# Gated rows transposed on VectorE in 32x32 squares with transfers inside SBUF, and the output's products moved behind the sixth product

## The chip, the cores and the metric

The kernel runs on one core of one Trainium2 chip. The metric is the device time of one execution in microseconds (us), the median of the runs. For a single execution the hardware profiler gives a trace, from which all the rows below come.

## The reference

One block of a network on 2048 rows of 512 columns, in f32: an attention part, then a gated part, each with a normalisation ahead and an addition to its input behind.

```python
h = x + _A_ref(_layernorm(x, axis=-1), A_wqkv, A_wo)
h2 = h + _B_ref(_layernorm(h, axis=-1), B_w_in, B_w_sp, B_b_sp, B_w_out)

def _B_ref(x, w_in, w_sp, b_sp, w_out):
    z = _gelu(jnp.einsum("bsd,df->bsf", x, w_in))
    z1 = z[..., :Fh]                                  # Fh = 688
    z2 = _layernorm(z[..., Fh:], axis=-1)
    g = jnp.einsum("ts,bsf->btf", w_sp, z2) + b_sp[None, :, None]
    return jnp.einsum("bsf,fd->bsd", z1 * g, w_out)
```

The change is in the last two lines: the product of w_sp (2048x2048) with z2 (2048x688), the gate z1 * g, and the product of the gated rows with w_out (688x512).

## The kernel before

All large products are made from fp16 halves: an f32 operand is split into a part rounded to fp16 (`hi`) and the rest (`lo`), and hi x hi, hi x lo and lo x hi are summed in PSUM (`mm3`, lines 106 to 109; their matmuls carry lines 107, 108 and 109 everywhere).

The last stage (lines 1413 to 1512) runs over eight pairs of row blocks, `p` = 0 to 7; a pair is the blocks p and p + 8 of 128 rows each (`w` = 0 and 1, "top" and "bottom"). In each pair:

- Seven products of one 1024-deep sum and 344 columns give g for both blocks (a Strassen-like scheme). They run in the order b11, t1, t2, b22, t3, b21, n4, each of 24 matmuls (`product`, which also asks for a left operand `op` eight products ahead, by SyncE). They accumulate in PSUM tiles A, C and B.
- VectorE and ScalarE combine the sums, GpSimd multiplies with z1. This makes the gated rows `pr`, two blocks of 688 columns in f32: right of top behind b22, right of bottom (`br`) behind t3, left of top behind b21, left of bottom (`bl`) behind n4.
- The columns are handled in two halves: half 0 is the columns 0 to 383, half 1 the rest. `level` finds each row's largest magnitude in a half (VectorE), `raise_` scales the half by a power of two (ScalarE, in place), `lower` makes the factors that undo it.
- The output's product needs the gated rows with columns along the partitions. `turn` transposes three 128x128 tiles on TensorE into PSUM, `split` reads them there into fp16 `pT` hi (ScalarE) and lo (VectorE), `multiply` makes one 128x512 output product from three tiles (9 matmuls for half 0, 8 for half 1) in a PSUM tile `acc`, `gather` scales it and adds it to the rows of h (VectorE), `store` writes them out.

The tiles `acc` come from a pool of two (`ps_o`, `bufs=2`). The order of instructions on each engine is the order of the code (a manual schedule), each engine takes its queue strictly in order, and semaphores connect the engines. In the code before, half 1 of a pair is turned behind its product n4, its output products (`multiply(1, w)`) stand behind the next pair's b11, followed there by the turn of half 0, whose output products stand behind the next pair's t1. The last pair has its own tail at lines 1497 to 1512, and it turns half 1 ahead of n4.

Of the kernel before, what the change touches and what calls it, by code (L numbers as in the profile page):

```python
# [8 lines left out]
F32 = mybir.dt.float32  # L9
F32R = mybir.dt.float32r  # L10
BF = mybir.dt.bfloat16
F16 = mybir.dt.float16
I32 = mybir.dt.int32
AF = mybir.ActivationFunctionType
# [5 lines left out]
P = 128  # L20
# [4 lines left out]
FH = 688  # L25
# [15 lines left out]
HF = 3 * P  # L41
# [18 lines left out]
def block_kernel(ctx: ExitStack, tc: tile.TileContext, x, wqkv, wo, w_in, w_sp4, b_sp, w_out, out):  # L60
# [7 lines left out]
    nc = tc.nc  # L68
# [26 lines left out]
    def split(hi, lo, src, eh=None, el=None):  # L95

        if eh == "act":
            nc.scalar.activation(hi, src, AF.Copy)  # L98
        elif eh == "pool":
            nc.gpsimd.tensor_copy(hi, src)  # L100
        else:
            nc.vector.tensor_copy(hi, src)
        back = hi if hi.dtype == F16 else hi.bitcast(F32)
        (nc.gpsimd if el == "pool" else nc.vector).tensor_sub(lo, src, back)  # L104
# [164 lines left out]
    with ExitStack() as pre:  # L269
# [244 lines left out]
        kf, accs, rest, measures = {}, [0], [], []  # L514
# [96 lines left out]
        for g in range(3):  # L611
            a, b = 4 * g, 4 * g + 4
# [54 lines left out]
        for j in range(24):  # L667
            b, n, i = 1 + j // 8, j // 2 % 4, 1 - j % 2
# [117 lines left out]
    with ExitStack() as at:  # L786
# [13 lines left out]
        def product(s, hg, qb, kb, p, t):  # L800

            r = slice(RG * t, RG * t + KM)
            nc.tensor.matmul(s, kst[hg % 2][r, p, kb * P:(kb + 1) * P],  # L803
                             qst[hg * NQ + qb][r, p, :], start=True, stop=True)
# [122 lines left out]
        def send():  # L927
            for i, key in enumerate(measured):
                nc.sync.dma_start(top_scr.rearrange("o (p i) -> (o p) i", i=4)[:, i:i + 1],
                                  sizes_of[key][:, :1])  # L930
# [112 lines left out]
        for n in range(0, len(units), 2):  # L1043
# [53 lines left out]
            for tok in PAIR if len(later) < 2 else ():  # L1097
                i = int(tok[-1]) if tok[-1].isdigit() else 0
# [16 lines left out]
                elif tok == "H":  # L1115
                    a = 0 if first else 256
# [47 lines left out]
    with ExitStack() as mid:  # L1164
# [5 lines left out]
        def turn(sb):  # L1170

            hn = hns.pop(sb)
            tp = pt.tile([P, DB, P], F32, name="tp")
            for d in range(DB):
                nc.tensor.transpose(tp[:, d, :], hn[:, d * P:(d + 1) * P], ident)
            hTs[sb] = [m2.tile([P, DB, P], F16, name=f"hT{i}") for i in range(2)]
            split(hTs[sb][0], hTs[sb][1], tp, "act")
# [107 lines left out]
    with ExitStack() as fin:  # L1285
# [3 lines left out]
        f2 = fin.enter_context(tc.tile_pool(name="fin_2", bufs=2))  # L1289
# [5 lines left out]
        def next_g():  # L1295
            banks[0] += 1
            return ps_g[(banks[0] - 1) // 2 % 2].tile([P, 512], F32, name="g")[:, :FC]

        TW = P // 2
# [38 lines left out]
        class Rows:  # L1338
# [26 lines left out]
            def lower(self, half, *which):  # L1365

                for w in which:
                    d = self.downs[half, w]
                    nc.vector.tensor_scalar(d, d, 2.0 ** -14, w_down, op0=ALU.mult, op1=ALU.mult)

            def turn(self, half, w):

                if half:
                    nc.gpsimd.tensor_copy(self.pr[:, w, FH:], self.pr[:, w, FH - TW:FH])
                tp = self.turned[half, w] = ps_t.tile([P, 512], F32, name="tp").rearrange(
                    "p (i t) -> p i t", t=P)
                for i in range(3):
                    c = min(HALVES[half].start + i * P, FH - TW)
                    nc.tensor.transpose(tp[:, i, :], self.pr[:, w, c:c + P], ident)

            def split(self, half, w):

                tp, n = self.turned.pop((half, w)), 3 - half
                if half not in self.pT:
                    self.pT[half] = [f2.tile([P, 2, 3, P], F16, name=f"pT{half}{i}") for i in range(2)]
                hi, lo = self.pT[half]
                nc.scalar.activation(hi[:, w], tp[:, :3], AF.Copy)
                nc.vector.tensor_sub(lo[:, w, :n], tp[:, :n], hi[:, w, :n])
                if half:
                    t = hi[TW:, w, n]  # L1390
                    nc.vector.tensor_sub(t, tp[TW:, n], t)
# [33 lines left out]
        with tc.manual_schedule(engines={E.PE, E.Activation, E.DVE, E.Pool, E.SP}):  # L1425
            wu = [f1.tile([P, 2 * 3, D], F16, name=f"wu{i}") for i in range(2)]
            raw_w = f1.tile([P, 2 * 3, D], F32, name="raw_w")
            w_top, w_low, w_up, w_down = [f1.tile([P, n], F32, name=f"w_{i}") for i, n in enumerate((6, 1, 1, 1))]
            nc.gpsimd.memset(raw_w[:, 2 * 3 - 1, :], 0.0)
            nc.sync.dma_start(raw_w[:, :5, :], w_out[:5 * P, :].rearrange("(i p) c -> p i c", p=P))  # L1430
            for r0 in (TW - fn, P - fn):
                nc.sync.dma_start(raw_w[r0:r0 + fn, 5, :], w_out[5 * P:, :])
            nxt = fetch(0)
            now = None
            for p in range(HB):
                (z1t, z1b, ht, hb), last = nxt, p + 1 == HB
                nxt = None if last else fetch(p + 1)
                before, now = now, Rows(p, (ht, hb))
                bt, bb = bias_up[:, p:p + 1], bias_up[:, p + HB:p + HB + 1]
                A, C, B = [next_g() for _ in range(3)]  # L1440
                p1, v, q5 = [f0.tile([P, FC], F32, name=n) for n in ("p1", "v", "q5")]
                left, right = now.pr[:, 0, :FC], now.pr[:, 0, FC:FH]
                bl, br = now.pr[:, 1, :FC], now.pr[:, 1, FC:FH]

                product(A, "b11")
                nc.scalar.activation(p1, A, AF.Identity, bias=bt)
                if p:
                    accs = [before.multiply(1, w) for w in range(2)]
                    for w in range(2):
                        before.turn(0, w)  # L1450
                        before.gather(1, w, accs[w])
                        before.split(0, w)
                    before.lower(0, 0, 1)
                product(C, "t1")
                nc.scalar.activation(q5, C, AF.Identity, bias=bb)
                if p:
                    accs = [before.multiply(0, w) for w in range(2)]
                    for w in range(2):
                        before.gather(0, w, accs[w])
                        before.store(w)  # L1460
                else:
                    weigh_w()
                product(A, "t2", False)
                nc.scalar.activation(v, A, AF.Identity, bias=bt)
                product(C, "b22", False)
                nc.vector.tensor_add(right, C, v)  # L1466
                nc.gpsimd.tensor_mul(right, right, z1t[:, FC:])  # L1467
                if not p:
                    measure_w()
                product(A, "t3", False)  # L1470
                nc.vector.tensor_add(br, A, q5)
                (nc.vector if last else nc.gpsimd).tensor_mul(br, br, z1b[:, FC:])
                now.level(1, 0, 1)
                now.raise_(1, 0, 1)
                product(B, "b21")
                nc.vector.tensor_add(left, B, p1)
                (nc.vector if last else nc.gpsimd).tensor_mul(left, left, z1t[:, :FC])
                if last:
                    now.level(0, 0)
                    for w in range(2):  # L1480
                        now.turn(1, w)
                        now.split(1, w)
                    now.lower(1, 0, 1)
                    now.raise_(0, 0)
                product(A, "n4", False)
                nc.vector.scalar_tensor_tensor(bl, A, bb, z1b[:, :FC], op0=ALU.add, op1=ALU.mult)
                if last:
                    now.level(0, 1)
                    now.raise_(0, 1)
                else:  # L1490
                    now.level(0, 0, 1)
                    for w in range(2):
                        now.turn(1, w)
                        now.split(1, w)
                    now.lower(1, 0, 1)
                    now.raise_(0, 0, 1)
            accs = [now.multiply(1, 0)]
            now.turn(0, 0)
            now.split(0, 0)
            accs.append(now.multiply(1, 1))  # L1500
            now.turn(0, 1)
            now.gather(1, 0, accs[0])
            now.split(0, 1)
            now.gather(1, 1, accs[1])
            now.lower(0, 0, 1)
            acc = now.multiply(0, 0)
            now.gather(0, 0, acc)
            now.store(0)
            acc = now.multiply(0, 1)
            for c in (slice(0, D // 2), slice(D // 2, D)):  # L1510
                now.gather(0, 1, acc, c)
                now.store(1, c)
# [29 lines left out]
```

## Time and profile before

| what | us |
|---|---|
| median of 3 runs (1726.46 to 1728.48) | 1726.86 |
| the profiled execution's own time | 1726.86 |
| its span, first to last instruction | 1725.10 |
| TensorE busy | 1708.8 (99%) |
| VectorE busy | 1438.4 (83%) |
| ScalarE busy | 1318.7 (76%) |
| GpSimd busy | 815.5 (47%) |

In the rows, PE is TensorE, DVE VectorE, ACT ScalarE, POOL GpSimd and SPq the queue of SyncE, which issues the transfers. A timeline row has the start, the duration, the engine, the line of the kernel, the instruction, the tile written and the tiles read, the shapes, and in brackets how long the engine had been idle and who ended that. A row by line has the count, the busy time and the mean of one in ns, then the idle time ahead. A row of a stretch has for each engine the busy time and the number of instructions in it, then the granted TensorE clock, the share of the DMA engines and GB/s. Matmul rows overlap, so TensorE's own pace is read from start to start. The last stage lies between 1455 and 1725 us.

### The profile page before, as it was taken

What the parts mean: (1) busy time and instruction counts of PE and PEld (TensorE: products, weight loads), DVE (VectorE), ACT (ScalarE), POOL (GpSimd) and SP (SyncE); (2) the same over time, 40 slices, a digit from 0 to 9 for tenths busy, and PEclk for the clock granted to TensorE, in tenths of its full rate; (3) what the DMA queues carried; (4) which work ended last, traced back from release to release, by engine and by line L of the source; (5) the groups of instructions that cost most, each with busy time, mean ns of one, the idle gap of its engine ahead of it and who ended that gap; (6) DMA issues with size and microseconds to landing.
All of it is one profiled execution on the core that took longest, in us unless ns stands there. A gap on an engine that the chain in (4) does not pass through costs nothing.

```text
span 1725.1 us, 36747 instructions
## 1 busy us (share of the span) xinstructions
PE 1708.8 (99%) x13583; PEld 653.4 (38%) x13583; DVE 1438.4 (83%) x3030; ACT 1318.7 (76%) x2598; POOL 815.5 (47%) x1076
## 2 busy tenths in 40 slices
PE   9999999999999999999999999999999999999999
PEld 4433222222222222222222222222216566666665
DVE  7688999999999999999999999999927886433234
ACT  4334999999999999999999999999994554221111
POOL 1231867776672267687677866400013766110010
PEclk9999999999999999999999999999999999999999
DMA  5534332342231234344345343300124464654540
GB/s 183 162 97 144 101 88 69 100 98 81 75 71 27 60 105 117 113 149 135 103 121 146 115 147 103 80 20 12 45 51 135 136 184 159 228 179 145 170 139 25
DMA packets 183932, 190.51 MB, mean 110 GB/s; under 512 B 65704, under 2 KB 134632, under 8 KB 183752
## 3 DMA queue, kind: packets, MB, share of 16 engines
q1 hardware_dynamic: 181448, 182.53, 36.2%
q10 hardware_dynamic: 2304, 5.64, 0.8%
q8 instruction: 106, 1.74, 0.4%
q14 instruction: 74, 0.61, 0.1%
HBM read 122.10 MB, written 65.93 MB: 109 GB/s over the span
## 4 chain that ended last, share of the span: by engine, by line
PE 76%; DVE 15%; DMA 3%; ACT 2%; issue 2%; POOL 2%; SPq 1%; DVEq 0%; ACTq 0%; POOLq 0%
PE pv L828 26%; PE s L803 17%; PE m L223 9%; DVE mx L228 7%; PE acc L107 4%; PE g L109 4%; PE g L108 4%; PE g L107 4%; PE acc L109 3%; PE acc L108 3%; DVE ab L237 1%; DMA rc<-r_scr 1%; DVE og L838 1%; DVE rs_t L124 1%; DVE rs_u L126 1%
## 5 line engine op out<-in xcount | busy, mean ns | idle before, releaser
L812 ACT ACTIVATE pt<-s 128x512 f32<-128x512 f32 x1968 | 1006.3, 637 | 5.1 <-PE m L223 4.0
L228 DVE TENSOR_REDUCE mx<-m 128x1 f32<-128x512 f32 x1510 | 947.5, 682 | 12.6 <-PE m L223 3.9
L803 PE MATMUL s<-qst,kst 50*128 50x512 f16 x2048 | 604.3, 379 | 0.2
L828 PE MATMUL pv<-pt,vst 128*32 128x256 f32 (+1 forms) x6056 | 598.1, 466 | 4.1 <-DVE og L838 1.3
L223 PE MATMUL m<-kst,qst 48*128 48x512 f16 x1510 | 452.4, 381 | 0.0
L803 PEld LDWEIGHTS <-kst 50*128 50x128 f16 x2048 | 131.9, 94 | 352.1 <-issue 323.7
L828 PEld LDWEIGHTS pv<-pt,vst 128*32 128x32 f32 x6056 | 119.5, 108 | 290.3 <-issue 276.9
L223 PEld LDWEIGHTS <-qst 48*128 48x128 f16 x2048 | 159.2, 93 | 173.7 <-issue 124.3
L223 PE MATMUL m<-uvs,qst 48*128 48x512 f16 x504 | 190.5, 380 | 0.3 <-DVE mx L228 0.3
L245 POOL TENSOR_SCALAR nm<-nm 128x16 f32<-128x16 f32 x32 | 6.6, 206 | 359.7 <-DVE nm L242 359.7
L237 DVE CUSTOM_DVE_ANT_0 ab<-m,ab 128x512 f32<-128x512 f32 x252 | 170.5, 677 | 2.7 <-ACT ab L233 2.7
L233 ACT ACTIVATE ab<-m 128x512 f32<-128x512 f32 x252 | 157.3, 624 | 16.5 <-PE m L223 15.8
L989 POOL TENSOR_TENSOR op<-raw,op 128x512 f16<-128x512 f32 x80 | 92.9, 1161 | 6.0
L1467 POOL TENSOR_TENSOR pr<-pr,z 128x344 f32<-128x344 f32 x8 | 7.3, 912 | 176.9 <-DVE pr L1466 173.0
L912 POOL TENSOR_TENSOR raw<-raw 128x512 f32<-128x512 f32 (+1 forms) x84 | 83.3, 991 | 6.7
L917 POOL TENSOR_TENSOR acc_sp<-acc_sp,raw 128x512 f32<-128x512 f32 x63 | 80.5, 1277 | 4.5
L107 PE MATMUL acc<-wi,hT 128*128 128x344 f16 x256 | 79.1, 309 | 1.4 <-ACT hT L98 1.4
L1362 ACT ACTIVATE pr<-pr,up 128x304 f32<-128x304 f32 (+1 forms) x32 | 17.0, 574 | 81.9 <-DVE up L1316 81.9
L109 PE MATMUL acc<-wi,hT 128*128 128x344 f16 x256 | 79.1, 309 | 0.3 <-DVE hT L104 0.3
L108 PE MATMUL acc<-wi,hT 128*128 128x344 f16 x256 | 79.1, 309 | 0.0
L1408 DVE SCALAR_TENSOR_TENSOR h<-acc,low,h 128x512 f32<-128x512 f32 (+1 forms) x33 | 24.1, 732 | 45.8 <-PE acc L109 32.5
L909 POOL TENSOR_SCALAR raw<-raw 128x512 f32<-128x512 f32 (+1 forms) x88 | 52.3, 594 | 19.5 <-DMA raw<-in_wqkv 12.2
(240 smaller groups left out, 2280.1 us busy)
## 6 DMA issues: line engine op xcount, KB each, us to landing
raw<-in_w_sp SPq DMA_DIRECT2D x128, 256.0 KB
s_scr<-op SPq DMA_DIRECT2D x64, 256.0 KB
op<-s_scr SPq DMA_DIRECT2D x32, 512.0 KB
a_scr<-op SPq DMA_DIRECT2D x48, 256.0 KB
op<-a_scr SPq DMA_DIRECT2D x24, 512.0 KB
o_scr<-og SPq DMA_DIRECT2D x64, 128.0 KB
qst<-q_scr SPq DMA_DIRECT2D x192, 32.0 KB
kst<-k_scr SPq DMA_DIRECT2D x48, 128.0 KB
```

The source lines that it names most:

```text
L107: nc.tensor.matmul(ps, lh, rh, start=first, stop=False, **kw)
L108: nc.tensor.matmul(ps, lh, rl, start=False, stop=False, **kw)
L109: nc.tensor.matmul(ps, ll, rh, start=False, stop=last, **kw)
L223: nc.tensor.matmul(acc, q[r, p, c], keys[r, p], start=True, stop=True)
L228: nc.vector.reduce_max(at(t, e if t else e - 1), acc, axis=AX.X)
L233: nc.scalar.activation(ab[0], acc, AF.Abs)
L237: nc.vector.tensor_tensor_reduce(ab[0], acc, ab[0], 0.5, LOW, ALU.add, ALU.max, at(0, 0))
L803: nc.tensor.matmul(s, kst[hg % 2][r, p, kb * P:(kb + 1) * P], qst[hg * NQ + qb][r, p, :], start=True, stop=True)
L812: nc.scalar.activation(pts[p, kb][:, t, :], s, AF.Exp, scale=scales_[hg // 2])
L828: nc.tensor.matmul(pv[0][32 * j:32 * j + 32, a:b], vst[hg % 2][:, c:c + 32], pts[j % 2, kb][:, j // 2, a:b], start=kb == 0, stop=kb == NB - 1,
L912: pool.tensor_mul(got[0] if n else acc, got[0], got[0])
L989: chores.append((lambda: pool.tensor_sub(t[0][:, 1], of(), t[0][:, 0]), TT))
```

## The change

For all pairs but the last, the transposition leaves TensorE and PSUM:

- `squares(half)` transposes the scaled rows on VectorE in squares of 32x32, from `pr` into an SBUF tile `squares`. In half 1 these are four instructions (two of 256 columns, two of 2x64), issued behind the scaling that follows t3; in half 0 one instruction of 768 columns, behind the scaling that follows n4.
- `send` puts the squares in their places with 16 transfers from SBUF to SBUF, each of 32 partitions with 384 elements, issued by SyncE into a tile `whole`.
- `hi` and `lo` split `whole` into the fp16 tiles: ScalarE copies 768 columns for each half (behind b22 of the next pair), VectorE subtracts with four instructions (behind t3 of the next pair, ahead of `level`).
- All four output products stand behind b21 of the next pair and ahead of n4, half 1 first; `store` stands behind n4.
- The last pair is turned by TensorE as before. Its `turn` of half 1 now stands between the two halves of pair 6's output products.

```diff
+            def squares(self, half):
+                if half:
+                    self.sq = f2.tile([P, 4, 2, 2, 3, 32], F32, name="squares", bufs=1)
+                t = self.sq[:, :, half]
+                if half:
+                    for w in range(2):
+                        nc.vector.transpose(t[:, :, w, :2].rearrange("p q i a -> p i q a"),
+                                            self.pr[:, w, HF:HF + 2 * P])
+                    for q in (0, 2):
+                        nc.vector.transpose(t[:, q:q + 2, :, 2].rearrange("p q w a -> p w q a"),
+                                            self.pr[:, :, FH - TW:FH])
+                else:
+                    nc.vector.transpose(t.rearrange("p q w i a -> p (w i) q a"), self.pr[:, :, :HF])
+            def send(self):
+                self.whole = f2.tile([P, 4, 2, 2, 3, 32], F32, name="whole", bufs=1)
+                for j in range(4):
+                    for q in range(4):
+                        nc.sync.dma_start(self.whole[32 * q:32 * q + 32, j], self.sq[32 * j:32 * j + 32, q])
+            def hi(self, half):
+                src = self.whole[:, :, half].rearrange("p j w i a -> p (w i) j a")
+                self.pT[half] = [f2.tile([P, 2, 3, P], F16, name=f"pT{half}{i}", bufs=1) for i in range(2)]
+                nc.scalar.activation(self.pT[half][0].rearrange("p w i (j a) -> p (w i) j a", a=32), src, AF.Copy)
...
                 product(A, "b11")
                 nc.scalar.activation(p1, A, AF.Identity, bias=bt)
-                if p:
-                    accs = [before.multiply(1, w) for w in range(2)]
-                    for w in range(2):
-                        before.turn(0, w)
-                        before.gather(1, w, accs[w])
-                        before.split(0, w)
-                    before.lower(0, 0, 1)
                 product(C, "t1")
...
                 (nc.vector if last else nc.gpsimd).tensor_mul(br, br, z1b[:, FC:])
+                if p:
+                    before.lo(1)
+                    before.lo(0)
                 now.level(1, 0, 1)
                 now.raise_(1, 0, 1)
+                if not last:
+                    now.squares(1)
                 product(B, "b21")
                 nc.vector.tensor_add(left, B, p1)
                 (nc.vector if last else nc.gpsimd).tensor_mul(left, left, z1t[:, :FC])
+                if p:
+                    accs = [before.multiply(1, w) for w in range(2)]
+                    for w in range(2):
+                        before.gather(1, w, accs[w])
...
+                if p:
+                    accs = [before.multiply(0, w) for w in range(2)]
+                    for w in range(2):
+                        before.gather(0, w, accs[w])
                 product(A, "n4", False)
...
                     now.level(0, 0, 1)
-                    for w in range(2):
-                        now.turn(1, w)
-                        now.split(1, w)
-                    now.lower(1, 0, 1)
                     now.raise_(0, 0, 1)
+                    now.squares(0)
+                    now.send()
```

On VectorE, in a middle pair, this is the queue from the addition behind t3 to the one behind n4 as it was (`pr<-g,q` is the addition behind t3, `pr<-g,p` the one behind b21):

```order
L1471 TENSOR_TENSOR pr<-g,q_23975 128x344
L1351 TENSOR_REDUCE low_24173<-pr 128x2
L1313 TENSOR_SCALAR low_24173<-low_24173 128x2
L1314 TENSOR_SCALAR low_24173<-low_24173 128x2
L1316 TENSOR_SCALAR up_24174<-low_24173 128x2
L1476 TENSOR_TENSOR pr<-g,p_23973 128x344
L1486 SCALAR_TENSOR_TENSOR pr<-g,fig_1843,z_23660 128x344
```

And this is the queue from the addition behind t3 to the first gather of an output product (`h<-acc`) in the changed kernel:

```order
L1508 TENSOR_TENSOR pr<-g,q_24284 128x344
L1410 TENSOR_TENSOR pT_24399<-whole,pT_24398 128x256 x2
L1412 TENSOR_TENSOR pT_24398<-whole,pT_24398 64x2x128
L1406 TENSOR_TENSOR pT_24402<-whole,pT_24401 128x768
L1351 TENSOR_REDUCE low_24436<-pr 128x2
L1313 TENSOR_SCALAR low_24436<-low_24436 128x2
L1314 TENSOR_SCALAR low_24436<-low_24436 128x2
L1316 TENSOR_SCALAR up_24437<-low_24436 128x2
L1378 STREAM_TRANSPOSE squares<-pr 128x2x4x32 x2
L1381 STREAM_TRANSPOSE squares<-pr 128x2x2x32 x2
L1518 TENSOR_TENSOR pr<-g,p_24282 128x344
L1451 SCALAR_TENSOR_TENSOR h_23666<-acc,low_24132,h_23666 128x512
```

Four subtractions stand ahead of the maximum, four transpositions ahead of the addition behind b21, and the gathers follow that addition.

On TensorE, before, at the border of two pairs the six transposes stand between n4 and b11:

```order
L108 MATMUL g<-n_1_20677,op 128x344
L109 LDWEIGHTS op
L109 MATMUL g<-n_0_20676,op 128x344
L1379 MATMUL tp<-ident,pr 128x128 x6
L107 LDWEIGHTS op
L107 MATMUL g<-b_0_20664,op 128x344
```

In the changed kernel they are gone there. This is the place behind b21 where the second output product ends and the third begins (pT_23790 is half 1, pT_23793 half 0):

```order
L1446 LDWEIGHTS pT_23790
L1446 MATMUL acc<-wu_23068,pT_23790 128x512
L107 LDWEIGHTS pT_23793
L107 MATMUL acc<-wu_23067,pT_23793 128x512
L108 LDWEIGHTS pT_23793
L108 MATMUL acc<-wu_23068,pT_23793 128x512
```

The output products of the two halves, which had the six transposes and t1 between them, now follow each other directly.

On SyncE, the 16 transfers stand behind the stores of the pair before and ahead of the loads for the next pair but one, in the changed kernel:

```order
L1161 DMA op<-a_4_scr 128x2048
L1454 DMA out_y<-h_23090 128x512
L1454 DMA out_y<-h_23092 128x512
L1391 DMA whole<-squares 32x384 x16
L1464 DMA z_23966<-z_scr 128x688
L1464 DMA z_23968<-z_scr 128x688
L1464 DMA h_23970<-h_scr 128x512
L1464 DMA h_23972<-h_scr 128x512
L1161 DMA op<-s_4_scr 128x2048 x4
```

The loads of z and h, which stood at the start of the pair behind the seventh `op`, now wait in the queue behind the squares.

More of the change, by code (lines that the diff above doesn't have):

```diff
@@ L1369, in lower, with lo @@
                     nc.vector.tensor_scalar(d, d, 2.0 ** -14, w_down, op0=ALU.mult, op1=ALU.mult)
+            def squares(self, half):
[20 more added lines that the diff above has]
+                nc.scalar.activation(self.pT[half][0].rearrange("p w i (j a) -> p (w i) j a", a=32), src, AF.Copy)
+            def lo(self, half):
+                src, (hi, lo) = self.whole[:, :, half], [
+                    t.rearrange("p w i (j a) -> p w i j a", a=32) for t in self.pT[half]]
+                if not half:
+                    lo, src, hi = [t.rearrange(f"p {d} -> p (w i) j a")
+                                   for t, d in ((lo, "w i j a"), (src, "j w i a"), (hi, "w i j a"))]
+                    nc.vector.tensor_sub(lo, src, hi)
+                    return
+                src = src.rearrange("p j w i a -> p w i j a")
+                for w in range(2):
+                    nc.vector.tensor_sub(lo[:, w, :2], src[:, w, :2], hi[:, w, :2])
+                t = hi[TW:, :, 2]
+                nc.vector.tensor_sub(t, src[TW:, :, 2], t)
             def turn(self, half, w):
@@ L1384, in split @@
                 if half not in self.pT:
-                    self.pT[half] = [f2.tile([P, 2, 3, P], F16, name=f"pT{half}{i}") for i in range(2)]
+                    self.pT[half] = [f2.tile([P, 2, 3, P], F16, name=f"pT{half}{i}", bufs=1) for i in range(2)]
                 hi, lo = self.pT[half]
@@ L1446, in block_kernel @@
                 nc.scalar.activation(p1, A, AF.Identity, bias=bt)
-                if p:
-                    accs = [before.multiply(1, w) for w in range(2)]
-                    for w in range(2):
-                        before.turn(0, w)
-                        before.gather(1, w, accs[w])
-                        before.split(0, w)
-                    before.lower(0, 0, 1)
                 product(C, "t1")
                 nc.scalar.activation(q5, C, AF.Identity, bias=bb)
-                if p:
-                    accs = [before.multiply(0, w) for w in range(2)]
-                    for w in range(2):
-                        before.gather(0, w, accs[w])
-                        before.store(w)
-                else:
+                if not p:
                     weigh_w()
@@ L1464, in block_kernel @@
                 nc.scalar.activation(v, A, AF.Identity, bias=bt)
+                if p:
+                    before.lower(1, 0, 1)
+                    before.lower(0, 0, 1)
                 product(C, "b22", False)
@@ L1467, in block_kernel @@
                 nc.gpsimd.tensor_mul(right, right, z1t[:, FC:])
-                if not p:
+                if p:
+                    before.hi(1)
+                    before.hi(0)
+                else:
                     measure_w()
@@ L1477, in block_kernel @@
                 (nc.vector if last else nc.gpsimd).tensor_mul(left, left, z1t[:, :FC])
+                if p:
+                    accs = [before.multiply(1, w) for w in range(2)]
+                    for w in range(2):
+                        before.gather(1, w, accs[w])
                 if last:
@@ L1484, in block_kernel @@
                     now.raise_(0, 0)
+                if p:
+                    accs = [before.multiply(0, w) for w in range(2)]
+                    for w in range(2):
+                        before.gather(0, w, accs[w])
                 product(A, "n4", False)
                 nc.vector.scalar_tensor_tensor(bl, A, bb, z1b[:, :FC], op0=ALU.add, op1=ALU.mult)
+                if p:
+                    for w in range(2):
+                        before.store(w)
                 if last:
@@ L1491, in block_kernel @@
                     now.level(0, 0, 1)
-                    for w in range(2):
-                        now.turn(1, w)
-                        now.split(1, w)
-                    now.lower(1, 0, 1)
                     now.raise_(0, 0, 1)
+                    now.squares(0)
+                    now.send()
             accs = [now.multiply(1, 0)]
```

## The prediction

> **What bounds the kernel now.** I read the page's busy shares first, then the busy time of each engine by stretch over the last stage (one stretch for each pair of row blocks), then the timeline of each engine inside one middle pair.
>
> ```profile
> span 1725.1 us, 36747 instructions
> PE 1708.8 (99%) x13583; PEld 653.4 (38%) x13583; DVE 1438.4 (83%) x3030; ACT 1318.7 (76%) x2598; POOL 815.5 (47%) x1076
> ```
>
> ```profile
> 1480.97:1514.10 33.13, 33.13 (x216) 21.12 (x215) 10.50 (x26) 5.47 (x12) 3.09 (x5) 1.00 0.53 172
> ```
>
> The program's own time in this execution is 1726.86 us around a span of 1725.1, and 1726.86 is also the median of the runs, so the sum below needs no shift. In the stage that is changed TensorE is busy for all 33.13 us of a pair at a granted clock of 1.00; VectorE for 10.5, ScalarE for 5.5, GpSimd for 3.1. So each us that leaves TensorE is a us gained, and each new wait of TensorE is a us lost, whichever engine causes it.
>
> **What goes.** TensorE's timeline shows the blocks of six transposes: a middle one, the first pair's first, and the last pair's, which stays.
>
> ```profile
> 1513.28 0.82 PE L1379 MATMUL tp<-ident,pr 128*128 128x128 f32 x6
> 1513.93 0.31 PE L107 MATMUL g<-b,op 128*128 128x344 f16 x1
> ...
> 1479.86 1.09 PE L1379 MATMUL tp<-ident,pr 128*128 128x128 f32 x6
> 1480.78 0.31 PE L107 MATMUL g<-b,op 128*128 128x344 f16 x1
> ...
> 1708.67 1.05 PE L1379 MATMUL tp<-ident,pr 128*128 128x128 f32 x6
> 1709.55 0.31 PE L107 MATMUL g<-n,op 128*128 128x344 f16 x1
> ```
>
> From start to start a block holds TensorE for 0.65 us; the first holds it 0.92, because it waits for its rows. Seven pairs lose two blocks each: 13 x 0.655 + 0.92 = 9.44 us. The last pair's block takes 0.88, that is 0.22 of waiting; in the change the products of pair 6 stand ahead of it and its rows are ready, so I count 0.22 more. **Gain: 9.66 us.** TensorE's other instructions are the same in number and kind. The copies to fp16 and the subtractions stay too, on other operands; GpSimd loses two small copies a pair, which nobody waited for.
>
> **What the transfers cost.** Each pair's 16 transfers can start when the second transposition is done. The rows of before, with the end of product n4, 1513.28, as zero:
>
> ```profile
> 1513.48 0.57 DVE L1486 SCALAR_TENSOR_TENSOR pr<-g,fig,z 128x344 f32<-128x344 f32 x1 [2.98 <-PE g L109]
> 1515.82 1.12 ACT L1362 ACTIVATE pr<-pr,up 128x384 f32<-128x384 f32 x2 [1.14 <-DVE up L1316]
> ...
> 1613.90 0.90 SPq L1421 DMA_DIRECT2D h<-h_scr  x2
> 1359.05 2.43 SPq L724 DMA_DIRECT2D rc<-r_scr  x4
> ...
> SPq L263 <- DMA m_scr<-mturned: 36.3, 32, 2.3
> ...
> L1212 ACT ACTIVATE z<-z,nb,rs_u x16: 959/961/962, 1309.3 to 1457.4; 128x688 f32<-128x688 f32 x16
> ```
>
> The rows are scaled at 3.66 and, with 0.96 for 768 columns, in squares at 4.7. No trace shows a transfer inside SBUF. An issue by SyncE takes 0.45 to 0.61 us (two in 0.90, four in 2.43); I take the former, since both sides are plain rows: 16 are issued by 12. A small transfer is waited for 36.3/32 = 1.1 us, at most 2.3, so the squares stand at about 13.5 to 14.5. ScalarE needs 0.96 x 768/688 = 1.07 for each fp16 copy and is done by 15.6 and 16.7. VectorE asks for them at 18.25 (five products of 3.50, then the addition). So they are **hidden, with 2.6 us to spare**; behind them on SyncE stand only the next loads, whose tiles are used a pair later. If an issue took over about 0.7 us the cover would be gone.
>
> **What the move costs.** The output's products now stand between b21 and n4, and they use two accumulators. Four products come in a row, so the third reuses the accumulator that VectorE's first gather empties. Before, over 3.5 us of another product lay between; now TensorE reaches it at once.
>
> ```profile
> 1506.28 0.31 PE L107 MATMUL g<-b,op 128*128 128x344 f16 x1
> 1509.78 0.31 PE L107 MATMUL g<-n,op 128*128 128x344 f16 x1
> ...
> 1517.43 0.38 PE L107 MATMUL acc<-wu,pT 128*128 128x512 f16 x1
> 1520.88 0.82 PE L1379 MATMUL tp<-ident,pr 128*128 128x128 f32 x6
> ```
>
> With b21's start (1506.28) as zero, TensorE does b21 until 3.50 and the first two output products until 3.50 + 3.45 = 6.95, where it wants the accumulator. VectorE's queue ahead of that gather is the matter:
>
> ```profile
> 1506.48 0.52 DVE L1471 TENSOR_TENSOR pr<-g,q 128x344 f32<-128x344 f32 x1 [2.91 <-PE g L109]
> 1508.02 0.79 DVE L1351 TENSOR_REDUCE low<-pr 128x2 f32<-128x608 f32 x1 [1.02 <-POOL pr L1472]
> 1509.98 0.52 DVE L1476 TENSOR_TENSOR pr<-g,p 128x344 f32<-128x344 f32 x1 [0.56 <-PE g L109]
> 1521.94 0.56 DVE L1388 TENSOR_TENSOR pT<-tp,pT 128x384 f16<-128x384 f32 x1 [1.82 <-ACT pT L1387]
> 1522.41 0.74 DVE L1408 SCALAR_TENSOR_TENSOR h<-acc,low,h 128x512 f32<-128x512 f32 x1
> ...
> 1507.07 0.91 POOL L1472 TENSOR_TENSOR pr<-pr,z 128x344 f32<-128x344 f32 x1 [2.51 <-DVE pr L1471]
> ...
> 1509.51 0.99 ACT L1362 ACTIVATE pr<-pr,up 128x304 f32<-128x304 f32 x2 [9.49 <-DVE up L1316]
> ```
>
> ```profile
> L1388 DVE TENSOR_TENSOR pT<-tp,pT 128x384 f16<-128x384 f32 x12 | 6.6, 552 | 11.2 <-ACT pT L1387 11.2
> L1388 DVE TENSOR_TENSOR pT<-tp,pT 128x256 f16<-128x256 f32 x12 | 5.1, 421 | 0.2
> L1391 DVE TENSOR_TENSOR pT<-tp,pT 64x128 f16<-64x128 f32 x12 | 3.5, 295 | 0.4
> ```
>
> - The addition of t3: 0.20 to 0.72.
> - `lo`, now here: three subtractions of 256 columns (0.42 each) and one of 768. From 256 to 384 columns the price rises by 0.13, so 768 cost 0.95. With gaps of 0.03: 0.75 to 3.06.
> - They have two operands in SBUF while GpSimd multiplies two operands in SBUF (0.91, from 0.79). What such a meeting does, the timeline of an earlier stage shows:
>
> ```profile
> 1335.60 0.83 POOL L1195 TENSOR_TENSOR b<-z,b 128x344 f16<-128x344 f32 x1
> 1335.71 1.09 DVE L1195 TENSOR_TENSOR b<-z,b 128x344 f16<-128x344 f32 x1
> 1336.40 1.18 POOL L1231 TENSOR_TENSOR z<-z,z 128x344 f32<-128x344 f32 x1
> ...
> 1446.38 0.52 DVE L1195 TENSOR_TENSOR b<-z,b 128x344 f16<-128x344 f32 x1 [1.92 <-ACT b L1194]
> ```
>
> VectorE's subtraction took 1.09 instead of 0.52 and ended 0.37 behind GpSimd's end (1336.43); GpSimd's next then ended 0.78 behind VectorE's. They take turns. Here the first subtraction runs until 1.17, GpSimd until 1.95, the second subtraction until 2.23 instead of 1.62: 0.6 lost, `lo` ends at 3.67. (Bounds: nothing, or the full 0.91.) [...]
> - Maximum, three small steps and the first scaling: 1508.02 to 1510.01 = 1.99 in the rows, so 3.70 to 5.69; the second scaling until 6.18.
> - The squares of half 1, two of 256 and two of 128 columns. The only transposition by VectorE in the trace is small:
>
> ```profile
> L259 DVE STREAM_TRANSPOSE mturned<-mparts x32: 199/201/211, 143.9 to 1252.2; 128x32 f16<-128x32 f16 x32
> ```
>
> 0.201 us for 32 columns is where the subtractions' line (0.295 at 128, 0.42 at 256) would put them, so I take that line: 2 x 0.42 + 2 x 0.30 = 1.44, though these are f32. Bounds: the line below, and 0.201 for every 32 columns, 4.8, above; I stay at the line, to which the row is nearest. [...] They end at 7.32, the second having waited for the second scaling.
> - Addition of b21 (0.52) and the gather (0.75): 8.65; TensorE starts 0.07 later, at 8.7. Two readers of PSUM may start 0.09 before the one ahead ends (1522.41 against 1522.50), which takes off 0.2.
>
> So TensorE waits from 6.95 until 8.5 to 8.7: **about 1.6 us, in each of the pairs 1 to 6**, 9.6 us in all. The fourth product finds its accumulator free (the second gather ends by 9.5, it starts at 10.5). The last pair has no squares, and its six transposes stand ahead of the third product: no wait. Sum: 1726.86 - 9.66 + 9.6 = **1726.8 us**.
>
> **Rivals.**
> - *The wait is shorter.* If GpSimd's product costs VectorE nothing and readers overlap, the wait is 0.9 us: 1726.86 - 9.66 + 5.4 = 1722.6. For it: an overlap of 0.09 in the rows; against it: the turn-taking above.
> - *No wait at all*, 1717.2: VectorE's queue would have to be 1.6 us shorter. Nothing in the rows does that; only an f32 transposition far below the line would.
> - *Squares of f32 at half the rate.* The trace has only f16. Twice 1.44 makes the wait 3.05 us: 1726.86 - 9.66 + 18.3 = 1735.5, slower. It ends on that side once the four take 0.55 us more than I count; the upper bound of 4.8 gives 5.0 us a pair, 1747.
> - *The transfers come late.* At 1.0 us an issue the squares stand at 22, `lo` starts 4 us later, GpSimd is out of the way by then: a wait of 5.0 us, some 1747, and a little more in the last pair. Against it: issues of 0.45 to 0.61.
>
> **How the numbers follow.** Forecast 0.42; shorter wait 0.20; no wait 0.06; slow squares 0.24; late transfers 0.08. About 0.2% (3.45 us) is what a measurement can tell from no change: the forecast is inside it, which gives 0.42 for the same, 0.26 for faster, 0.32 for slower. The range leaves out no wait, late transfers and the far end of slow squares: 1721.5 to 1737. The forecast's own range, with waits of 1.2 to 2.1, is 1724.5 to 1730.
>
> **What would show it.** In the changed profile a middle pair should last 31.8 us plus one gap of TensorE, between the second and third output product, ended by VectorE's gather. The subtractions beside GpSimd's product should show one of about 0.9 to 1.1 instead of 0.42; the transpositions 0.42, 0.30 and 0.96; ScalarE's wait for the squares should end 3 us or more ahead of VectorE's. No gap there, a gap ahead of the first output product, or transpositions off the line would make the prediction wrong.

## The result and the profile after

The median went from 1726.86 us (11 runs, 1725.97 to 1728.48) to 1722.97 us (11 runs, 1721.56 to 1723.39): a ratio of 0.9977, with a 95% interval of 0.9969 to 0.9985. The change makes the kernel faster by 0.23%, 3.9 us. The forecast of 1726.8 (no change) did not come; the rival "the wait is shorter", 1722.6, did.

The profiled execution took 1722.97 us itself. Its page, and the busy times of the engines over two middle pairs (from the gating of `bl` to the next one):

```profile
span 1721.2 us, 36670 instructions
PE 1701.2 (99%) x13499; PEld 644.4 (37%) x13499; DVE 1453.0 (84%) x3051; ACT 1317.5 (77%) x2584; POOL 813.6 (47%) x1062
```

```profile
1512.78:1545.55 32.77, 32.00 (x204) 19.76 (x203) 12.96 (x29) 5.33 (x9) 2.85 (x3) 1.00 0.54 191
1545.55:1578.32 32.77, 32.00 (x204) 19.77 (x203) 12.96 (x29) 5.32 (x9) 2.85 (x3) 1.00 0.54 190
```

A pair lasts 32.77 us instead of 33.13. TensorE has 12 matmuls fewer in it, and is no longer busy all the time: 0.77 us of each of these two pairs are idle at a granted clock that is still 1.00. VectorE took over 2.5 us of work (12.96 instead of 10.50). Where the idle time lies, TensorE's timeline around the border between the second and the third output product shows, and the waits of the last stage show how often:

```profile
1569.59 0.38 PE L1446 MATMUL acc<-wu,pT 128*128 128x512 f16 x1
1570.73 0.38 PE L107 MATMUL acc<-wu,pT 128*128 128x512 f16 x1 [0.77 <-DVE h L1451]
```

```profile
ACT pT L1397 <- DMA whole<-squares: 34.0, 6, 6.6
...
PE acc L107 <- DVE h L1451: 5.1, 6, 1.0
```

The place is the one forecast: the third output product waits for the accumulator that VectorE's gather (line 1451) empties, six times, once in each of the pairs 1 to 6. Since matmul rows overlap, the gap is best read from start to start: a matmul of 512 columns starts 0.21 behind the one ahead, here it was 1.14, so 0.93 us are lost (32.77 less the 31.84 that a pair takes without the gap, below, is 0.93 too).

VectorE's queue in the same pair; b21 starts at 1562.85, which is the zero of the prediction's steps:

```profile
1563.05 0.52 DVE L1508 TENSOR_TENSOR pr<-g,q 128x344 f32<-128x344 f32 x1 [2.91 <-PE g L109]
1563.49 1.47 DVE L1410 TENSOR_TENSOR pT<-whole,pT 128x256 f16<-128x256 f32 x2
1564.97 0.42 DVE L1412 TENSOR_TENSOR pT<-whole,pT 64x256 f16<-64x256 f32 x1
1565.42 0.96 DVE L1406 TENSOR_TENSOR pT<-whole,pT 128x768 f16<-128x768 f32 x1
1566.30 0.78 DVE L1351 TENSOR_REDUCE low<-pr 128x2 f32<-128x608 f32 x1
...
1568.36 0.89 DVE L1378 STREAM_TRANSPOSE squares<-pr 128x256 f32<-128x256 f32 x2 [0.67 <-ACT pr L1362]
1569.16 0.46 DVE L1381 STREAM_TRANSPOSE squares<-pr 128x128 f32<-128x128 f32 x2
1569.55 0.48 DVE L1518 TENSOR_TENSOR pr<-g,p 128x344 f32<-128x344 f32 x1
1569.95 1.39 DVE L1451 SCALAR_TENSOR_TENSOR h<-acc,low,h 128x512 f32<-128x512 f32 x2
```

The reader is to see two things: the order is the forecast one (subtractions, maximum, squares, addition, gathers), and most of the long rows start a little (0.07 to 0.09) ahead of the end of the row above them. The duration of a group is that of its first start to its last end.

The transpositions and the transfers by line (ns: least, median, most), and SyncE's and ScalarE's rows for the same pair:

```profile
L1378 DVE STREAM_TRANSPOSE squares<-pr x14: 445/445/447, 1479.1 to 1667.3; 128x256 f32<-128x256 f32 x14
```

```profile
L1381 DVE STREAM_TRANSPOSE squares<-pr x14: 269/269/270, 1479.9 to 1667.9; 128x128 f32<-128x128 f32 x14
```

```profile
L1391 SPq DMA_DIRECT2D whole<-squares x112: 507/589/1600, 1485.7 to 1691.4; - x112
```

```profile
1550.05 10.01 SPq L1391 DMA_DIRECT2D whole<-squares  x16
```

```profile
1561.64 1.58 ACT L1397 ACTIVATE pT<-whole 128x768 f16<-128x768 f32 x2 [5.04 <-DMA whole<-squares]
```

Product n4 of the pair ahead ended at 1545.35. Sixteen issues take SyncE 10.0 us, 0.63 each; the squares stand at 16.3 behind n4's end, the fp16 copies at 17.9, and VectorE's first subtraction starts at 18.14. That first subtraction needs only the first of the two copies, 0.83 of the 1.58, which stands at 17.1: in this pair the transfers are hidden with 1.0 us to spare.

In two of the pairs, 1 and 5, they are not hidden. VectorE's first subtraction waits there for ScalarE's copy, and TensorE's gap is the longer by 0.23:

```profile
1497.39 1.58 ACT L1397 ACTIVATE pT<-whole 128x768 f16<-128x768 f32 x2 [6.56 <-DMA whole<-squares]
1498.27 1.15 DVE L1410 TENSOR_TENSOR pT<-whole,pT 128x256 f16<-128x256 f32 x2 [0.47 <-ACT pT L1397]
1505.20 0.38 PE L107 MATMUL acc<-wu,pT 128*128 128x512 f16 x1 [1.00 <-DVE h L1451]
...
1629.45 1.29 DVE L1410 TENSOR_TENSOR pT<-whole,pT 128x256 f16<-128x256 f32 x2 [0.32 <-ACT pT L1397]
1636.52 0.38 PE L107 MATMUL acc<-wu,pT 128*128 128x512 f16 x1 [1.00 <-DVE h L1451]
```

In both, the first gather starts 7.13 behind the start of the addition of t3, in the pair above 6.90. The rest of the late start is made good by a shorter meeting with GpSimd (1.15 and 1.29 for the two subtractions instead of 1.47).

### The profile page after: what moved, and what is told of

Same layout as the page of the kernel before. It is cut to its first block, busy times and chain, and to the rows that moved or that the text cites. A ratio compares the mean times of both kernels' runs of the same rounds, so it can differ in the third digit from the quotient of the medians.

```text
span 1721.2 us, 36670 instructions
## 1 busy us (share of the span) xinstructions
PE 1701.2 (99%) x13499; PEld 644.4 (37%) x13499; DVE 1453.0 (84%) x3051; ACT 1317.5 (77%) x2584; POOL 813.6 (47%) x1062
## 4 chain that ended last, share of the span: by engine, by line
PE 69%; DVE 17%; DMA 3%; issue 3%; ACT 2%; SPq 2%; POOL 2%; DVEq 0%; ACTq 0%; POOLq 0%
PE pv L828 26%; PE s L803 17%; PE m L223 9%; DVE mx L228 7%; PE acc L107 3%; PE acc L109 3%; PE acc L108 3%; PE g L108 2%; PE g L107 2%; PE g L109 2%; DVE ab L237 1%; DMA rc<-r_scr 1%; DVE og L838 1%; SPq L1391 1%; DVE rs_t L124 1%
## 5 line engine op out<-in xcount | busy, mean ns | idle before, releaser
L894 POOL TENSOR_SCALAR raw<-raw,figs 128x512 f32<-128x512 f32 (+1 forms) x84 | 55.8, 668 | 8.6 <-ACT pt L812 7.7
```

## The experiments

The theory: the gain is the 9.66 us of the removed transposes, and all that is given back is TensorE's wait for the first gather, which is late because VectorE has the squares of half 1 and `lo`, slowed by GpSimd, ahead of it. The rivals: the move of the output's products costs by itself; the transfers cost; the removed transposes bring less than 9.66.

### The squares behind the gathers

```diff
-                if not last:
-                    now.squares(1)
                 product(B, "b21")
...
                         before.gather(1, w, accs[w])
+                if not last:
+                    now.squares(1)
```

> Change against the changed kernel: the four transpositions of half 1 stand behind the two gathers of half 1, no longer ahead of the addition behind b21. Theory (TensorE waits 0.94 us a pair, pairs 1 to 6, because the third output product reuses the accumulator that VectorE's first gather empties late): the gather comes about 1.3 us earlier than TensorE needs by 0.9, so the gap goes; 1722.97 - 6 x 0.94 = 1717.3 us, a middle pair lasts 31.83 us. Rival (the gap has another cause, such as the fp16 tiles being late): the gap stays or moves, 1722 to 1723 us.

Measured: 1716.75 us (5 runs, 1716.63 to 1717.56), a ratio to the kernel before of 0.9943 (0.9929 to 0.9956). The busy times of two middle pairs and VectorE's timeline in one of them:

```profile
1512.27:1544.11 31.84, 31.84 (x204) 19.74 (x203) 12.96 (x30) 5.33 (x9) 2.85 (x3) 1.00 0.55 196
1544.11:1575.94 31.83, 31.83 (x204) 19.76 (x203) 12.96 (x29) 5.32 (x9) 2.85 (x3) 1.00 0.55 196
```

```profile
1566.14 0.51 DVE L1516 TENSOR_TENSOR pr<-g,p 128x344 f32<-128x344 f32 x1
1566.83 0.75 DVE L1451 SCALAR_TENSOR_TENSOR h<-acc,low,h 128x512 f32<-128x512 f32 x1 [0.18 <-PE acc L1446]
1568.56 0.75 DVE L1451 SCALAR_TENSOR_TENSOR h<-acc,low,h 128x512 f32<-128x512 f32 x1 [0.97 <-PE acc L1446]
1569.23 0.76 DVE L1378 STREAM_TRANSPOSE squares<-pr 128x256 f32<-128x256 f32 x2
1569.91 0.46 DVE L1381 STREAM_TRANSPOSE squares<-pr 128x128 f32<-128x128 f32 x2
```

The same instructions, one step later: now VectorE waits for TensorE before each gather (0.18 and 0.97 in brackets), and TensorE is busy for all 31.84 us of the pair. 31.84 is 33.13 less two blocks of transposes (1.30), to 0.01. The whole gain is 9.73 us of 9.66 counted. Each pair's wait was the only thing given back.

### Another accumulator, nothing moved

```diff
-                acc = ps_o.tile([P, 512], F32, name="acc")
+                if half == 0 and self.p < HB - 2:
+                    acc = ps_t.tile([P, 512], F32, name="tp")
+                else:
+                    acc = ps_o.tile([P, 512], F32, name="acc")
```

> Change against the changed kernel: the output products of half 0 of pairs 0 to 5 take their accumulators from the pool of two that the transposes on TensorE used, so the third product does not reuse the first one's; VectorE's order is as in the changed kernel. Theory (reuse of the accumulator): no gap behind the second output product although the gather stays as late as it is; 1717.3 us, a middle pair 31.83 us. Rival (TensorE waits for something else that VectorE makes, such as the low halves of half 0): the gap of 0.94 us stays, 1723 us.

Measured: 1716.73 us (5 runs, 1716.26 to 1716.97), ratio 0.9943 (0.9929 to 0.9956). VectorE's timeline, from the addition of t3 to the gathers:

```profile
1560.55 0.52 DVE L1511 TENSOR_TENSOR pr<-g,q 128x344 f32<-128x344 f32 x1 [2.91 <-PE g L109]
...
1567.45 1.39 DVE L1454 SCALAR_TENSOR_TENSOR h<-acc,low,h 128x512 f32<-128x512 f32 x2
1569.44 0.75 DVE L1454 SCALAR_TENSOR_TENSOR h<-tp,low,h 128x512 f32<-128x512 f32 x1 [0.61 <-PE tp L109]
```

The first gather starts 6.90 behind the addition of t3, exactly as in the changed kernel (1569.95 less 1563.05). VectorE is as late as ever; only TensorE no longer needs its tile, and the time falls to that of the run above. So the reuse of the accumulator is shown to be the whole link: neither the squares nor the late gather cost anything without it.

### GpSimd's product on VectorE

```diff
-                (nc.vector if last else nc.gpsimd).tensor_mul(br, br, z1b[:, FC:])
+                nc.vector.tensor_mul(br, br, z1b[:, FC:])
```

> Change against the changed kernel: VectorE instead of GpSimd multiplies the right half of the bottom rows with z1 in all pairs. Theory (the second of the four subtractions loses 0.60 us because GpSimd's product of two SBUF operands runs then): VectorE's queue gains an instruction of 0.52 to 0.55 and loses the 0.60; the gap stays at 0.9 us, 1722.5 to 1723.2 us, and each subtraction of 256 columns takes 0.42. Rival (the two subtractions are slow for another reason, such as their operands' patterns): 1.47 for the two stays, the gap grows to 1.5, 1726.3 us.

Measured: 1721.31 us (7 runs, 1720.72 to 1722.20), ratio 0.9971 (0.9959 to 0.9982). Its VectorE timeline, and GpSimd's row of the changed kernel for the same product:

```profile
1561.91 0.52 DVE L1508 TENSOR_TENSOR pr<-g,q 128x344 f32<-128x344 f32 x1 [2.91 <-PE g L109]
1562.46 0.52 DVE L1509 TENSOR_TENSOR pr<-pr,z 128x344 f32<-128x344 f32 x1
1562.90 0.75 DVE L1410 TENSOR_TENSOR pT<-whole,pT 128x256 f16<-128x256 f32 x2
```

```profile
1563.65 1.02 POOL L1509 TENSOR_TENSOR pr<-pr,z 128x344 f32<-128x344 f32 x1 [2.46 <-DVE pr L1508]
```

Without GpSimd beside them the two subtractions take 0.75 instead of 1.47: the meeting costs VectorE 0.72 us, and GpSimd 0.11 (1.02 instead of 0.91). VectorE thus loses most of the length that GpSimd's instruction has in the kernel before, 0.72 of 0.91. VectorE now does the product itself, which lengthens its queue by 0.55 (1561.91 to 1562.46), so the gap of TensorE shrinks only a little, to 32.61 less 31.84 = 0.77 a pair. The product also moves the first subtraction back far enough that it no longer waits for ScalarE's copies in any pair: the six gaps have 0.62 of idle time on average and 0.6 in the longest, and the two longer ones are gone. All waits for the gather fall from 5.1 to 3.7 us. The expectation, 1722.5 to 1723.2 us, missed this: it counted the meeting at 0.60 instead of 0.72 and knew nothing of the two longer gaps. The gain on the changed kernel is 1.4 us by the waits and 1.7 us by the medians.

### The move without the squares

The kernel before, with its transposes left on TensorE and all output products behind b21:

```diff
                 if p:
-                    accs = [before.multiply(1, w) for w in range(2)]
                     for w in range(2):
                         before.turn(0, w)
-                        before.gather(1, w, accs[w])
                         before.split(0, w)
...
                 nc.vector.tensor_add(left, B, p1)
...
+                if p:
+                    accs = [before.multiply(1, w) for w in range(2)]
+                    for w in range(2):
+                        before.gather(1, w, accs[w])
...
+                if p:
+                    accs = [before.multiply(0, w) for w in range(2)]
+                    for w in range(2):
+                        before.gather(0, w, accs[w])
                 product(A, "n4", False)
```

> The kernel before with one part of the change alone: all output products behind b21 as in the changed kernel, the transposes left on TensorE at their places. Theory (the gain is the transposes' time on TensorE, the loss is VectorE's longer queue ahead of the gather; the move by itself costs nothing): no gap, a middle pair lasts 33.14 us as before; 1726.86 less 0.2 us in the last pair, 1726.4 to 1726.9 us. Rival (the move by itself brings the wait): a gap of 0.9 us a pair, 1732 us.

Measured: 1726.12 us (11 runs, 1725.57 to 1726.53), ratio 0.9996 (0.9987 to 1.0005). Two gatings of `bl`, one pair apart:

```profile
1546.13 0.57 DVE L1487 SCALAR_TENSOR_TENSOR pr<-g,fig,z 128x344 f32<-128x344 f32 x1 [2.75 <-PE g L109]
...
1579.28 0.58 DVE L1487 SCALAR_TENSOR_TENSOR pr<-g,fig,z 128x344 f32<-128x344 f32 x1 [2.75 <-PE g L109]
```

A pair lasts 33.15 us, as before (33.13). Four output products in a row on two accumulators cost nothing as long as VectorE's queue has neither squares nor late subtractions ahead of the gathers. The move alone is no loss and no gain; the rival falls.

### Each transfer in two

```diff
-                        nc.sync.dma_start(self.whole[32 * q:32 * q + 32, j], self.sq[32 * j:32 * j + 32, q])
+                        for half in range(2):
+                            nc.sync.dma_start(self.whole[32 * q:32 * q + 32, j, half],
+                                              self.sq[32 * j:32 * j + 32, q, half])
```

> Change against the changed kernel: each of the 16 transfers inside SBUF is split into two of half the columns, 32 a pair with the same bytes. Theory (SyncE's time for an issue, 0.63 us, sets when the squares stand, and their cover ends about 0.3 us later): the issues take 20 us instead of 10, ScalarE's copies end 10 us later, VectorE's first subtraction starts about 9.8 us later than now; TensorE then waits inside the first output product (about 7 us) and again for the accumulator (about 3 us): 9 us more in each of the pairs 1 to 6 and about 8 in the last, 1723 + 62 = about 1785 us. Rival (bytes or the time of landing set it, not the count): about 1723 us, the issues still 10 us.

Measured: 1786.08 us (2 runs, 1785.13 and 1787.03), ratio 1.0343 (1.0323 to 1.0364). SyncE's row, TensorE's first output product, and the busy times of the engines from there on:

```profile
1567.88 21.31 SPq L1392 DMA_DIRECT2D whole<-squares  x32
```

```profile
1591.49 0.61 PE L107 MATMUL acc<-wu,pT 128*128 128x512 f16 x1 [7.14 <-ACT pT L1399]
```

```profile
1592.00:1596.00 4.00, 4.00 (x11) 1.41 (x10) 3.18 (x8) 1.11 (x3) 0.00 (x0) 0.50 0.99 330
1596.00:1600.00 4.00, 3.97 (x16) 1.57 (x15) 2.71 (x7) 0.04 (x1) 0.92 (x1) 0.83 1.02 414
1600.00:1606.00 6.00, 6.00 (x39) 3.60 (x38) 1.91 (x3) 0.00 (x0) 0.00 (x0) 1.00 0.83 332
```

Twice as many transfers of half the bytes take 21.3 us instead of 10.0: SyncE pays for the issue (0.67 each), not for the bytes. The cover is gone, and TensorE waits 7.14 us at the first output product (6.3 to 7.4 in the seven pairs), where the changed kernel has no gap. A second loss follows: the granted clock is 0.50 and 0.83 in the next two stretches of 4 us. The time came out as expected (about 1785), but not by the sum expected: the second wait, for the accumulator, was counted at about 3 us in the pairs 1 to 6 and was 0.5 to 1.1 in five of them and under 0.2 in one. The lowered clock, which was not counted, took its place: it stretched the first two output products by some 2 us in each of those five pairs (an estimate: VectorE's rows put the third product some 6.5 us behind the first, where two products at full clock take 3.45; the wait is taken off), and by 2.9 us in the remaining one, the pair shown (its row above lasts 0.61 instead of 0.38). The rival "late transfers" is a real mechanism, and the changed kernel stands at its edge: 1.0 us short of it in the pair shown, 0.47 and 0.32 us inside it in the pairs 1 and 5.

### The squares of half 1 twice

`squares(1)` is done a second time, into the same tile (`squares` gets an argument for that, not shown):

```diff
                     now.squares(1)
+                    now.squares(1, now.sq)
```

> Change against the changed kernel: VectorE makes the four transpositions of half 1 twice in a row, into the same tile. This sets the price of the rival with transpositions at half the rate. Theory (each us in VectorE's queue ahead of the first gather is a us of TensorE in the pairs 1 to 6): the four take 1.26 us from start to end, the gap grows from 0.93 to 2.2 us, a middle pair lasts 34.0 us, 1722.97 + 6 x 1.26 = 1730.5 us. Rival (part of the queue has slack): less than half of it, below 1727 us.

Measured: 1730.28 us (10 runs, 1729.30 to 1733.83), ratio 1.0022 (1.0012 to 1.0032). VectorE's timeline, and TensorE's row at the end of the gap in another pair:

```profile
1573.17 0.89 DVE L1378 STREAM_TRANSPOSE squares<-pr 128x256 f32<-128x256 f32 x2 [0.67 <-ACT pr L1362]
1573.98 0.46 DVE L1381 STREAM_TRANSPOSE squares<-pr 128x128 f32<-128x128 f32 x2
1574.37 0.73 DVE L1378 STREAM_TRANSPOSE squares<-pr 128x256 f32<-128x256 f32 x2
1575.02 0.46 DVE L1381 STREAM_TRANSPOSE squares<-pr 128x128 f32<-128x128 f32 x2
1575.40 0.48 DVE L1519 TENSOR_TENSOR pr<-g,p 128x344 f32<-128x344 f32 x1
```

```profile
1610.62 0.38 PE L107 MATMUL acc<-wu,pT 128*128 128x512 f16 x1 [2.04 <-DVE h L1451]
```

The second set takes 1575.40 less 1574.37 = 1.03 us, not the 1.26 that I took from the first set, which contains a wait for the second scaling. A middle pair is longer by just that: 33.80 instead of 32.77. Whatever VectorE does there reaches TensorE one for one. Six times 1.03 is 6.2 us; the medians differ by 7.3. The profiled execution (1733.83, the longest) shows a further loss: behind two of its six gaps the granted clock fell, as in the stretch that follows the row above:

```profile
1610.60:1614.00 3.40, 3.38 (x9) 1.25 (x9) 0.62 (x1) 0.00 (x0) 0.30 (x1) 0.55 0.99 399
```

The mean granted clock was below 1.000 (0.998 or 0.999) in five of the ten executions, and these are the five longest. The other five, 1729.30 to 1729.99 us, lie 6.6 us above the changed kernel by their median. So the lowered clock goes with about 0.7 of the 7.3 us. That the median came so near the 1730.5 expected is partly luck: the second set was counted too long, and the clock was not counted.

## Why the prediction was right in its mechanism and wrong in a size

- **The gain, 9.66 us: right.** Without the wait it is 9.73 us (squares behind the gathers) and 9.75 us (another accumulator). The first block, counted at 0.92, left no gap either.
- **The transfers, "hidden, with 2.6 us to spare": the spare was 1.0 us in the pair shown and missing in two others.** The issue was taken at 0.45 us, from the lower of two rows; it took 0.63, slightly over the upper (0.61). The squares stood at 16.3 instead of 13.5 to 14.5, and the first copy, though shorter than counted (0.83 instead of 1.07), at 17.1 instead of 15.6. In the pairs 1 and 5 VectorE waited for that copy, which cost TensorE 0.23 us each, 0.5 in all, where the prediction had nothing. Its sign that ScalarE's wait for the squares ends 3 us or more ahead of VectorE's did not come: it was 1.85 in the pair shown (1561.64 against 1563.49) and 0.88 in pair 1.
- **The wait, "about 1.6 us, in each of the pairs 1 to 6": this is the term that was mis-sized.** It is 0.93 in four of the pairs and 1.16 in two (idle 0.77 to 0.79, and 1.00, each with the 0.16 that the matmul rows overlap), 6.1 us in all instead of 9.6. By the medians it is 9.73 less 3.89, 5.8 us. The place, the count and the cause are as forecast; the chain on VectorE was counted too long, by its own steps with b21's start as zero:

| step | forecast, end | measured, end |
|---|---|---|
| addition of t3 | 0.72 | 0.72 |
| `lo`, with GpSimd beside it | 3.67 | 3.53 |
| maximum, small steps, first scaling (measured: where the squares start) | 5.69 | 5.51 |
| squares of half 1 | 7.32 | 6.77 |
| addition of b21 and first gather, TensorE starts | 8.5 to 8.7 | 7.88 |

- The durations were nearly all right: subtractions 0.42 and 0.96 (0.42 and 0.95 counted), transpositions 0.445 and 0.269 (0.42 and 0.30), the addition 0.48 (0.52). GpSimd's turn cost 0.72, where 0.6 was counted. What failed was the joint between rows. I put a gap of 0.03 behind each instruction, and an overlap of 0.09 only at the last readers of PSUM, for the lower end of 8.5. In the trace six long rows start 0.07 to 0.09 ahead of the end of the one above: the first subtraction (1563.49 against 1563.57), the maximum (1566.30 against 1566.38), the two transpositions of 128 columns (the first at 1569.16 against 1569.25), the addition (1569.55 against 1569.62) and the gather (1569.95 against 1570.03). The third and fourth subtraction do not (1564.97 against 1564.96, 1565.42 against 1565.39). Four transpositions last 1.26 from first start to last end, with a wait inside, where their durations alone give 1.43. Six joints at some 0.1 less are about 0.65 of the 0.84 us between 8.72, the durations and gaps added up, and 7.88.
- **The rivals.** "The wait is shorter" gave its time (0.9 us, 1722.6), but partly by luck: of its two conditions only one held. The rows overlap, at more joints than it counted, while GpSimd's product did cost VectorE its turn. The measured time lies outside the forecast's own range, 1724.5 to 1730. Squares of f32 at half the rate are refuted by the rows of the transpositions (0.445 and 0.269 us, where twice the count would be 0.84 and 0.60). No wait at all came in two versions, at 1716.7 against the 1717.2 worked out for it. Of the late transfers, above.

Two versions beat both kernels, the squares behind the gathers and the other accumulator, at 0.9943 (0.9929 to 0.9956); there is no difference between them, since in both TensorE is busy throughout the pair.

## What to carry to other kernels

Where products that shared their accumulators with long gaps between them are moved together, count the queue of the engine that empties the first one, and give the third product another tile or put the emptying ahead of work that nobody waits for yet. When a chain on one engine is added up, take the distances from start to start in a dense part of the trace, not durations plus a gap: a tenth of a microsecond at each of six joints was most of the difference between no change and a gain here. Where work is hidden behind something, price it by the upper row, and look at every pair: a spare counted at 2.6 us was 1.0 in one pair and missing in two others.

## What the runs showed of the hardware

- A transfer of 32 partitions inside SBUF takes SyncE 0.59 us (median) to issue, and 0.63 from one to the next in the pair shown; with half the bytes 0.67. Loads next to it take less: the four of `op` stand in SyncE's timeline of the changed kernel for 2.07 us.

```profile
1560.16 1.00 SPq L1464 DMA_DIRECT2D z<-z_scr  x2
1561.20 0.90 SPq L1464 DMA_DIRECT2D h<-h_scr  x2
1562.21 2.07 SPq L1161 DMA_DIRECT2D op<-s_scr  x4
```

Why the transfers inside SBUF cost more was not tried, nor a second queue for them.

- VectorE transposes f32 in squares in 0.445 us for 256 columns and 0.269 for 128, about 1.4 ns a column between them; f32 shows no penalty to speak of against the subtractions of the same width (0.42 and 0.295).
- TensorE's granted clock fell to about a half behind a wait of 7.14 us in `transfers_doubled` (0.50 over the 4 us from 1592 on, 0.83 over the next 4), and in the profiled execution of `squares_twice` behind two of six waits of 1.8 to 2.7 us: 0.68 over 3.4 us behind that of 2.67, and 0.55 over 3.4 us behind that of 2.04. Behind one of 2.03 it stayed at 1.00. Behind waits of 0.8 to 1.0, in the changed kernel, it did not fall: all 11 executions have a mean of 1.000. Why there was a drop behind 2.04 us and none behind 2.03 stays open.
